# A quarter of the first product by Strassen's seven products from block 3 on, its weight sums on GpSimd, k of three tiles scaled by ScalarE

## The chip, the cores and the metric

The kernel runs on one core of a Trainium2 chip. A core has a matrix engine (PE; its weight loads are shown apart as PEld), a vector engine (DVE), a scalar engine (ACT), a general engine (GpSimd, POOL in the profile), and a queue engine (SP) that issues most DMAs. Each engine works through its own list of instructions in order, and semaphores order the engines against each other. The metric is the device time of one execution in microseconds, as the median of several runs.

## What is computed

A retention layer (attention with a decaying state) feeds a two-layer MLP with a parametric ReLU (PReLU). 4 batches, 8 heads, 768 positions, 64 values a head; 512 features, 2048 hidden ones; all inputs and the output in f32.

```python
for t in range(S):
    state = gamma[None, :, None, None] * state + np.einsum('bhd,bhe->bhde', k[:, :, t], v[:, :, t])
    y[:, :, t] = scale * np.einsum('bhd,bhde->bhe', q[:, :, t], state)
x = y.transpose(0, 2, 1, 3).reshape(B * S, H * D)          # 3072 x 512
h = x @ w_in                                               # the first product
g = np.maximum(h, 0.0) + alpha * np.minimum(h, 0.0)        # PReLU
out = g @ w_out                                            # the second product
```

## The kernel before, in words

Positions are cut into 24 tiles ("units") of 128; four units make a block of 512 tokens, and there are six blocks (n = 0 to 5). The program is written out by hand: a manual schedule, in which the order of the Python calls is the order on each engine. The two MLP products are Python generators that yield after each matmul; `tick(gen, m)` lets one go on by m matmuls, and between ticks other work is put into the queues. So the order around the change is set by the main loop at the end of the kernel alone.

Attention of one unit: `load` (L118) brings q, k and v to SBUF by SP's queue. `scaled` (L124) multiplies k or q by the decay factors from f32 to f16 (`kq`), on GpSimd as one instruction (L139) or on ACT as eight, one a head (L131). `turn` (L164) transposes `kq` by DMA to `kt`; `cast` (L152, L154) makes v f16. `prep` does all four for a unit on GpSimd. On PE, `scores` (L236) and `states` (L196) work on two units at once. On DVE, `masked` (L250) masks the scores, and `sums` (L211, L217) adds to the running state, whose decay is a multiply on GpSimd (L219). `out_first` and `out_second` (L295) make the outputs, which ACT and DVE copy to `xT`, the tokens of the next block as the first product reads them (L598, L601, L602).

The first product of a block (`ffn1`, L622) makes 16 hidden tiles of 128 x 512 tokens, four matmuls of 512 columns each. ACT makes relu(-h) (L631), and DVE's one instruction makes g from it and the PSUM bank (L632), into `gt`. The PSUM banks of these tiles take turns among four.

The second product from block 1 on (`seven`, L789) is Strassen's scheme: seven products of 16 matmuls of 256 columns instead of eight. It needs sums of `w_out` quarters (`wsum`, made once) and sums of `gt` quarters: `g_sums(n, part, which, eng)` (L739), in f16, 128 x 1024 an instruction, two parts for each of four sums. Sums 0 and 1 are chained and are DVE's; the third product needs sum 1, the fourth sum 0, the fifth sum 2, the seventh sum 3. GpSimd makes most of sums 2 and 3. Each has a tile of its own (`gs0` to `gs3`). Products leave PSUM by ACT copies (L807) and DVE adds (L819), and `out` is stored by SP.

Within block n's second product stands the attention of block n + 1: scores and states of the first pair of units, T_OUT1 matmuls, their outputs and the next pair's scores and states, T_OUT2 matmuls, that pair's outputs, and the rest of the matmuls. In `chain`, DVE does state sum, masks and state sum of a pair, with a `g_sums` on GpSimd or DVE between. All four units of block n + 1 are prepared by GpSimd during the first product of block n. Block 0 and the start are arranged otherwise and aren't touched; block 1's first product is done in two halves (L650, L664) in the midst of block 0's end.

## Time and profile before

| what | us |
|---|---|
| median of 3 runs | 198.95 |
| lowest and highest | 198.77, 200.19 |
| the profiled execution | 198.51 |
| its span in the profile | 196.5 |
| PE busy in it | 190.3 |
| DVE, ACT, POOL busy | 151.1, 98.5, 119.8 |

In the profile an instruction is named by its line, its engine, and tile written <- tiles read. The lines are those of the kernel before. In the timeline the first column is the start in us from the span's start, the second the duration of the group; x2 says that two equal ones are merged. In the groups by line the numbers behind the first bar are busy us and mean ns of one, those behind the second the idle time ahead of them.

### The profile page before, as it was taken

How to read it: one execution, taken by the hardware profiler on the slowest of the kernel's cores; microseconds unless marked ns; L12 is line 12 of the kernel's file. 1: busy time of each engine (PE TensorE's matmuls, PEld its weight loads, DVE VectorE, ACT ScalarE, POOL GpSimd, SP SyncE). 2: the span in 40 equal slices, each digit the busy share in tenths (PEclk: the TensorE clock that was granted, in tenths of full speed). 3: DMA queues.
4: the chain of work that ended last, by engine and by line, in shares of the span. 5: the costliest groups of instructions: out<-in, count | busy, mean ns of one | idle time of the engine just before them, and what ended most of it. 6: DMA issues, size and time to landing. Idle time of an engine off the chain costs nothing.

```text
span 196.5 us, 6280 instructions
## 1 busy us (share of the span) xinstructions
PE 190.3 (97%) x2632; PEld 128.9 (66%) x2632; DVE 151.1 (77%) x259; ACT 98.5 (50%) x192; POOL 119.8 (61%) x134
## 2 busy tenths in 40 slices
PE   7988999999999999999999999999999999999993
PEld 5757544558668888644888544888544888444882
DVE  2597989164989998589988589976689985789913
ACT  3378663238677925466333467234476234566110
POOL 3378989999999276994097992197971290040000
PEclk9999999999999999999999999999999999999999
DMA  5999999999998499999999999982660011300014
GB/s 157 330 358 389 407 388 329 337 332 206 209 226 188 89 291 219 226 295 257 213 228 208 286 171 251 253 208 78 180 141 0 3 57 55 109 0 3 0 53 160
DMA packets 92746, 38.75 MB, mean 197 GB/s; under 512 B 70176, under 2 KB 88624, under 8 KB 92720
## 3 DMA queue, kind: packets, MB, share of 16 engines
q1 hardware_dynamic: 91440, 37.36, 74.1%
q10 hardware_dynamic: 1280, 1.01, 1.6%
q8 instruction: 20, 0.33, 0.7%
q14 instruction: 6, 0.05, 0.1%
HBM read 27.35 MB, written 6.29 MB: 171 GB/s over the span
## 4 chain that ended last, share of the span: by engine, by line
PE 81%; DVE 9%; SPq 2%; DMA 2%; POOL 2%; issue 1%; ACT 1%; POOLq 0%
PE hps L622 33%; PE ops L789 28%; PE ops L717 5%; PE hps L650 5%; DVE gt L664 4%; SPq L342 2%; DMA qu<-in_q_dram 2%; DVE gs L739 2%; PE ops L686 2%; PE ya L524 1%; POOL gs L739 1%; PE ya L295 1%; DVE um L496 1%; PE yb L295 1%; PE sca L236 1%
## 5 line engine op out<-in xcount | busy, mean ns | idle before, releaser
L622 PE MATMUL hps<-xT,win 128*128 128x512 f16 x304 | 66.4, 379 | 0.0
L632 DVE SCALAR_TENSOR_TENSOR gt<-hm,small,hps 128x512 f16<-128x512 f32 x76 | 55.4, 745 | 8.6 <-ACT hm L631 3.5
L631 ACT ACTIVATE hm<-hps 128x512 f32<-128x512 f32 x76 | 45.4, 597 | 27.5 <-PE hps L622 27.5
L622 PEld LDWEIGHTS <-win 128*128 128x128 f16 x304 | 29.7, 98 | 34.8
L789 PEld LDWEIGHTS <-gs 128*128 128x128 f16 x320 | 30.9, 98 | 4.2 <-DVE gs L739 0.3
L139 POOL TENSOR_TENSOR kq<-kqs,tab 128x512 f16<-128x512 f32 x30 | 30.7, 1047 | 0.5 <-DMA kqs<-in_k_dram 0.3
L789 PE MATMUL ops<-wsum,gs 128*128 128x256 f16 x240 | 27.9, 273 | 0.1
L219 POOL TENSOR_TENSOR t<-ss,tab 128x256 f16<-128x256 f32 x13 | 8.4, 644 | 28.6 <-DVE ss L217 28.6
L789 PEld LDWEIGHTS <-gt 128*128 128x128 f16 x240 | 22.7, 98 | 3.4 <-DVE gt L632 0.3
L739 POOL TENSOR_TENSOR gs<-gt 128x1024 f16<-128x1024 f16 x7 | 14.9, 2130 | 14.7 <-DVE gt L632 14.7
L807 ACT ACTIVATE kept<-ops 128x512 f32<-128x512 f32 x15 | 9.0, 597 | 23.3 <-PE ops L789 23.3
L664 DVE SCALAR_TENSOR_TENSOR gt<-hm,small,hps 128x256 f16<-128x256 f32 x40 | 17.1, 476 | 4.3 <-ACT hm L659 4.2
L819 DVE TENSOR_TENSOR os<-ops,kept 128x512 f32<-128x512 f32 (+1 forms) x17 | 10.6, 626 | 11.3 <-ACT kept L807 6.3
L789 PE MATMUL ops<-wout,gt 128*128 128x256 f16 x160 | 18.5, 273 | 0.0
L650 PE MATMUL hps<-xT,win 128*128 128x256 f16 x160 | 18.3, 273 | 0.0
L650 PEld LDWEIGHTS <-win 128*128 128x128 f16 x160 | 15.4, 98 | 2.4
L659 ACT ACTIVATE hm<-hps 128x512 f32<-128x512 f32 x20 | 11.9, 599 | 5.7 <-PE hps L650 4.0
L739 POOL TENSOR_TENSOR gs<-gt,gs 128x1024 f16<-128x1024 f16 x5 | 10.6, 2129 | 3.9 <-DVE gs L739 3.9
L717 PE MATMUL ops<-wout,gt 128*128 128x512 f16 x48 | 11.4, 380 | 0.0
L394 ACT ACTIVATE ukT<-trb 128x512 f16<-128x512 f16 (+1 forms) x7 | 4.5, 657 | 11.6 <-PE trb L385 11.6
L789 PE MATMUL ops<-wsum,gt 128*128 128x256 f16 x80 | 10.2, 273 | 0.0
L356 POOL TENSOR_TENSOR ukq<-ku,tab 128x512 f16<-128x512 f32 x6 | 6.1, 1042 | 5.9 <-DMA ku<-in_k_dram 5.9
(107 smaller groups left out, 268.7 us busy)
## 6 DMA issues: line engine op xcount, KB each, us to landing
out_dram<-os SPq DMA_DIRECT2D x20, 256.0 KB, 3.2
wi<-in_moe_w_in_dram SPq DMA_DIRECT2D x8, 512.0 KB, 7.7
wo<-in_moe_w_out_dram SPq DMA_DIRECT2D x8, 512.0 KB, 8.7
kqs<-in_k_dram SPq DMA_DIRECT2D x16, 256.0 KB, 4.3
kqs<-in_q_dram SPq DMA_DIRECT2D x16, 256.0 KB, 4.4
vs<-in_v_dram SPq DMA_DIRECT2D x16, 256.0 KB, 4.6
ku<-in_k_dram SPq DMA_DIRECT2D x4, 256.0 KB, 4.2
qu<-in_q_dram SPq DMA_DIRECT2D x4, 256.0 KB, 4.6
```

The source lines that it names most:

```text
L139: eng.tensor_tensor(out=kqs[u][:, a].rearrange("p i r d -> p r i d"), in0=staged[u][nm].rearrange("p (r i) d -> p r i d", i=4), in1=tab[:, ...
L622: nc.tensor.matmul(out=hps, lhsT=w_in_all[:, hp, 128 * ft : 128 * ft + 128], rhs=xT[n][:, :, hp, :], start=(hp == 0), stop=(hp == 3),)
L631: nc.scalar.activation(out=hm, in_=hps, func=RELU, bias=0.0, scale=-1.0)
L632: nc.vector.scalar_tensor_tensor(out=gt_at(n, ft, slice(0, TB)), in0=hm, scalar=oma_sb[:, ft : ft + 1], in1=hps, op0=MULT, op1=ADD,)
L650: nc.tensor.matmul(out=hps[:, 256 * (ft - f0) : 256 * (ft - f0) + 256], lhsT=w_in_all[:, hp, 128 * ft : 128 * ft + 128], rhs=xT[n][:, half ...
L659: nc.scalar.activation(out=hm, in_=hps, func=RELU, bias=0.0, scale=-1.0)
L664: nc.vector.scalar_tensor_tensor(out=gt_at(n, f, to), in0=hm[:, at], scalar=oma_sb[:, f : f + 1], in1=hps[:, at], op0=MULT, op1=ADD,)
L717: nc.tensor.matmul(out=banks[tq], lhsT=gt_at(n, ft, slice(128 * tq, 128 * tq + 128)), rhs=w_out_all[:, ft, :], start=(ft == 0), stop=(ft = ...
L739: eng.tensor_tensor(out=out, in0=a, in1=b, op=op)
L789: nc.tensor.matmul(out=bk[:, 256 * t : 256 * t + 256], lhsT=a[:, f, 128 * t : 128 * t + 128], rhs=w[:, f, :], start=first and f == 0 and ( ...
L807: nc.scalar.activation(out=t, in_=bank, func=COPY, bias=0.0, scale=1.0)
L819: nc.vector.tensor_tensor(out=os_sb[:, at], in0=x[at.start // 256][:, at], in1=y[:, at], op=op)
```

## The change

From block 3 on the first product is done by `ffn1_mix`. It takes the hidden tiles 0, 1, 8 and 9 (a quarter of 16) by Strassen's seven products: 7 x 4 matmuls of 256 columns instead of 16 of 512. The other 12 tiles are done as before (`full`). The list MIX gives the order of the parts (0, i) and the full tiles (0). Some products add up in the same PSUM bank; three are kept in SBUF by ACT and added to by DVE (`add`). The PReLU of three of the four quarters is done from SBUF: relu by ACT, a multiply and an add by GpSimd (`ends`); the last one is done by ACT and DVE as in `full`.

It needs four sums of `w_in` quarters (`win_sum`, 128 x 1024 each, once, all on GpSimd: two ahead of block 1's second product, two during block 2's first) and four sums of `xT` (`x_sum`, 128 x 512, each block, two on DVE and two on GpSimd). Their tiles take the place of `gs2` and `gs3`, so `g_sums` 2 and 3 now overwrite parts of `gt`.

The order of other work changes with it. The first part of sum 0 of `gt` goes from DVE to GpSimd in blocks 3 to 5, the first part of sum 2 from GpSimd to DVE in block 5, and T_OUT1 is 46 instead of 44. `prep` is gone: block 2 calls its parts itself; from then on the q and k of the next block's first three units are scaled during the second product ahead (q by GpSimd, k by ACT), v is cast by ACT, and only the fourth unit is scaled by GpSimd in the mix. Loads stand behind that unit's transpose.

The diff, cut to its core:

```diff
-    T_OUT1, T_OUT2 = 44, 46
+    T_OUT1, T_OUT2 = 46, 46
...
-                sbp.tile([128, HF, 256], F16, tag=f"gs{i}", bufs=1, name=f"gs{n}{i}") for i in range(4)
+                sbp.tile([128, HF, 256], F16, tag=f"gs{i}", bufs=1, name=f"gs{n}{i}") for i in range(2)
...
-            minus(eng, sm[2][:, f], gt[:, f, t0], gt[:, f, t1])
+            minus(eng, gt[:, f, t1], gt[:, f, t0], gt[:, f, t1])
         else:
-            minus(eng, sm[3][:, f], gt[:, f8, t0], sm[1][:, f])
+            minus(eng, gt[:, f8, t0], gt[:, f8, t0], sm[1][:, f])
...
+    def win_sum(i, eng):
+        if not wins:
+            wins.append(sbp.tile([128, 2, 2, 512], F16, tag="gs2", bufs=1, name="wins0"))
+        if i == 2:
+            wins.append(sbp.tile([128, 2, 2, 512], F16, tag="ukq", bufs=2, name="wins1"))
+        a = [[w_in_all[:, 2 * l : 2 * l + 2, 1024 * j : 1024 * j + 512] for l in range(2)] for j in range(2)]
...
+    MIX = [(0, 1), (0, 2), 0, (0, 5), (0, 6), 0, (0, 7), 0, 0, (0, 4), (0, 3)] + 8 * [0]
...
+        def part(r, i):
...
+            if i in (1, 6, 7):
+                t = sbp.tile(
+                    [128, 512], FP, tag="um1" if i == 6 else "um0", bufs=2, name="kept"
+                )
+                nc.scalar.activation(out=t, in_=bk[r, "b"], func=COPY, bias=0.0, scale=1.0)
+                h[r, i] = t
+            if i in (2, 7, 3):
+                add(r, {2: 1, 7: 7, 3: 6}[i], at if i != 7 else "c")
+            if i == 4:
+                b = bk[r, "b"]
+                prelu(r, relu(b, "hm"), b, 1, 0)
+
+        def add(r, i, at):
+            nc.vector.tensor_tensor(out=h[r, i], in0=bk[r, at], in1=h[r, i], op=ADD)
+            later.append((at_step[0], r, i))
...
+        def ends():
+            while later:
+                _, r, i = later.pop(0)
+                row, half = {1: (0, 0), 7: (1, 1), 6: (0, 1)}[i]
+                hm = relu(h[r, i], "uv")
...
+                nc.gpsimd.tensor_tensor(
+                    out=hv,
+                    in0=hv,
+                    in1=oma_sb[:, f : f + 2].unsqueeze(2).to_broadcast([128, 2, 256]),
+                    op=MULT,
+                )
+                nc.gpsimd.tensor_tensor(
+                    out=gt_at(n, slice(f, f + 2), slice(256 * half, 256 * half + 256)),
+                    in0=hv,
+                    in1=v,
+                    op=ADD,
+                )
+
+        for s, step in enumerate(steps):
+            at_step[0] = s
+            yield from part(*step) if step else full()
+            if later and s - later[0][0] >= (3 if later[0][2] == 1 else 2):
+                ends()
+            if s == len(steps) - 4:
+                g_sums(n, 0, 0, nc.gpsimd if rounds == 1 else nc.vector)
+            if s == len(steps) - 2:
+                g_sums(n, 0, 1, nc.vector)
+        g_sums(n, 0, 2, nc.gpsimd if n + 1 < NBLK else nc.vector)
...
     cast(10, A)
     cast(11, A)
+    win_sum(0, G)
+    win_sum(1, G)
 
     for n in range(1, NBLK):
...
-            g_sums(n, 0, 2, nc.gpsimd)
+            g_sums(n, 0, 2, G)
+            win_sum(2, G)
+            win_sum(3, G)
+            for _ in gen:
+                pass
+        elif n > 2:
+            gen = ffn1_mix(n, MIX, 1)
+            tick(gen, 8)
+            flush(late_stores)
+            if more:
+
+                scaled(u0 + 3, "k", G)
+                scaled(u0 + 3, "q", G)
+                turn(u0 + 3)
+            for u in range(u0 + UB, min(u0 + 2 * UB, NU)):
+                load(u)
...
             if n > 1:
-                chain(pa, pq, (1, 2), None)
+                chain(pa, pq, [(1, 2, G)])
                 tick(gen, T_OUT1)
+                g_sums(n, 0, 3, G)
+                for u in nxt[0:1]:
+                    scaled(u, "k", A)
             else:
-                g_sums(n, 1, 3, nc.gpsimd)
                 tick(gen, 33)
-                chain(pa, pq, None, None)
-                g_sums(n, 0, 2, nc.vector)
-                g_sums(n, 1, 2, nc.vector)
+                chain(pa, pq)
+                g_sums(n, 1, 3, G)
+                g_sums(n, 0, 2, V)
+                g_sums(n, 1, 2, V)
                 tick(gen, 27)
...
+            tick(gen, 6)
+            for u in nxt[0:2]:
+                cast(u, A)
+            for u in nxt[1:2]:
+                scaled(u, "k", A)
+                scaled(u, "q", G)
+                turn(u)
+            for u in nxt[2:3]:
+                scaled(u, "q", G)
+            tick(gen, T_OUT2 - 6 if n > 1 else 23)
             out_first(pb, z=[ps("za"), ps("zb")])
             out_second(pb)
+            for u in nxt[2:3]:
+                scaled(u, "k", A)
+                turn(u)
+            tick(gen, 7)
+            if n > 1:
+                x_sum(n + 1, 0)
+                x_sum(n + 1, 1)
+                x_sum(n + 1, 2, G)
+                x_sum(n + 1, 3, G)
```

More of the change, by code (lines that the diff above doesn't have):

```diff
@@ L842, in seven @@
         yield from product(c, sm[0], wsum[0], True)
-        yield from product(b, sm[2], wsum[2])
+        yield from product(b, A(1, 0), wsum[2])
         u3 = kept(b, "um1")
@@ L851, in seven @@
         if end:
-            gen = product(c, sm[3], W(1, 1))
+            gen = product(c, A(0, 1), W(1, 1))
             for _ in range(HF):
@@ L859, in seven @@
         else:
-            yield from product(c, sm[3], W(1, 1))
+            yield from product(c, A(0, 1), W(1, 1))
             store()
             late_stores.append(put(0, 1, c, u2))
+    wins, xsum = [], []
+    def win_sum(i, eng):
[4 more added lines that the diff above has]
+        a = [[w_in_all[:, 2 * l : 2 * l + 2, 1024 * j : 1024 * j + 512] for l in range(2)] for j in range(2)]
+        x, y, op = (
+            (lambda: (a[1][0], a[1][1], ADD)),
+            (lambda: (wins[0][:, 0], a[0][0], SUB)),
+            (lambda: (a[0][0], a[1][0], SUB)),
+            (lambda: (a[0][1], wins[0][:, 1], SUB)),
+        )[i]()
+        minus(eng, wins[i // 2][:, i % 2], x, y, op=op)
@@ new lines, in x_sum @@
+    def x_sum(n, i, eng=nc.vector):
+        if not xsum:
+            xsum.append(sbp.tile([128, 4, 2, 256], F16, tag="gs3", bufs=1, name="xsum"))
+        t = xsum[0]
+        b = [[xT[n][:, j, 2 * l : 2 * l + 2, :] for j in range(2)] for l in range(2)]
+        x, y = (
+            (b[0][1], b[0][0]),
+            (b[1][1], t[:, 0]),
+            (b[1][1], b[0][1]),
+            (b[1][0], t[:, 1]),
+        )[i]
+        minus(eng, t[:, i], x, y)
+    MIX = [(0, 1), (0, 2), 0, (0, 5), (0, 6), 0, (0, 7), 0, 0, (0, 4), (0, 3)] + 8 * [0]
@@ L1124 @@
             for i in range(UB):
[L1125 to L1130 removed]
+                scaled(u0 + i, "k", G)
+                scaled(u0 + i, "q", G)
+                turn(u0 + i)
+                cast(u0 + i, G)
+                for u in ((), (0,), (), (1, 2, 3))[i]:
+                    load(u0 + u + UB)
                 tick(gen, (14, 14, 6, 16)[i])
                 if i in (1, 2):
[L1133 to L1134 removed]
+                    g_sums(n, 0, i - 1, V)
+            g_sums(n, 0, 2, G)
[13 more added lines that the diff above has]
+                load(u)
             for _ in gen:
```

126 lines of the change are left out of this document (97 added, 29 removed).

## The prediction

> **What bounds the kernel now.** I read the page's table of engines first, then the busy time by stage, then the chain of waits.
>
> ```profile
> span 196.5 us, 6280 instructions
> PE 190.3 (97%) x2632; PEld 128.9 (66%) x2632; DVE 151.1 (77%) x259; ACT 98.5 (50%) x192; POOL 119.8 (61%) x134
> ```
> ```profile
> 63.00:80.30 17.30, 17.25 (x386) 14.71 (x385) 15.40 (x30) 9.11 (x24) 10.73 (x10) 1.00 0.86 208
> ...
> 94.10:109.26 15.16, 15.16 (x362) 13.34 (x362) 12.29 (x23) 4.99 (x12) 9.62 (x10) 1.00 1.04 212
> 109.26:123.07 13.81, 13.81 (x73) 6.14 (x74) 11.92 (x18) 8.96 (x15) 9.29 (x10) 1.00 1.15 239
> ```
> ```profile
> 94.80 4.91 PE ops L789 x44
> 99.71 0.15 PE ya L295 x2
> ...
> 109.26 13.81 PE hps L622 x64
> ```
> The stage rows give the length, then the busy us of PE, PEld, DVE, ACT and POOL, then the granted clock. PE is never idle from block 1 on, at clock 1.00. So only fewer PE cycles can shorten the run, and every new PE wait lengthens it by its full size. A first product (L622) takes 13.81 us, 0.2158 per 128x512 matmul; the second product takes 4.91/44 = 0.1116 per 128x256 matmul.
>
> **One fact decides: DVE and GpSimd exclude each other.** Here are single sums, first on DVE (start, duration), then what GpSimd ran meanwhile.
>
> ```profile
> 32.36 2.02 DVE L739 TENSOR_TENSOR wsum<-wout 128x2048 f16<-128x2048 f16 x1
> ...
> 72.75 1.70 DVE L739 TENSOR_TENSOR gs<-gt 128x1024 f16<-128x1024 f16 x2
> ...
> 90.29 1.00 DVE L739 TENSOR_TENSOR gs<-gt 128x1024 f16<-128x1024 f16 x1
> ...
> 103.60 1.11 DVE L739 TENSOR_TENSOR gs<-gt,gs 128x1024 f16<-128x1024 f16 x1
> ...
> 119.23 0.68 DVE L739 TENSOR_TENSOR gs<-gt 128x1024 f16<-128x1024 f16 x1
> ```
> ```profile
> 10.28 1.41 POOL L356 TENSOR_TENSOR ukq<-qu,tab 128x512 f16<-128x512 f32 x1
> ...
> 31.26 2.04 POOL L356 TENSOR_TENSOR ukq<-ku,tab 128x512 f16<-128x512 f32 x2 [0.37 <-DMA ku<-in_k_dram]
> 33.26 3.02 POOL L356 TENSOR_TENSOR ukq<-qu,tab 128x512 f16<-128x512 f32 x2
> ...
> 72.92 0.99 POOL L219 TENSOR_TENSOR t<-ss,tab 128x256 f16<-128x256 f32 x1 [0.99 <-DVE ss L217]
> 75.39 0.61 POOL L219 TENSOR_TENSOR t<-ss,tab 128x256 f16<-128x256 f32 x1 [1.48 <-DVE ss L217]
> ...
> 88.61 2.13 POOL L739 TENSOR_TENSOR gs<-gt 128x1024 f16<-128x1024 f16 x1
> ...
> 103.54 0.62 POOL L219 TENSOR_TENSOR t<-ss,tab 128x256 f16<-128x256 f32 x1
> ```
> A sum of 1024 takes 0.68 on DVE with GpSimd idle (119.23). At 90.29 it took 1.00: GpSimd's sum ran to 90.74, 0.45 later, and DVE lost 0.32. At 103.60 GpSimd ran 0.56 longer and DVE lost 0.43. The loss is the overlap less 0.13 both times: DVE stands until GpSimd's instruction is done. It works the other way too: 0.99 instead of 0.61 at 72.92, behind DVE's 72.75 to 73.43; and at 33.26 the pair takes 3.02 where the pair before it took 2.04. That last place also shows who comes next: GpSimd's multiplies stood back to back, and DVE's sum got in between two of them; at 72.75 GpSimd got in between two DVE sums. So they take turns. The Trainium skill, "SBUF — State Buffer", section "SBUF: two separate sides", says that a DVE instruction with two SBUF inputs and a GpSimd instruction that reads SBUF exclude each other for the whole instruction. By that rule, without the 0.13, my seven or so blocked instructions would add up to 0.9 us more; the trace agrees on the exclusion and gives the 0.13, so I keep the trace's.
>
> DVE's PReLU (hm and a PSUM bank) is not held up: in these stretches of L632 alone, GpSimd is busy in the first and idle in the second, and DVE's share is 0.76 and 0.77.
> ```profile
> 139.00:145.00 6.00, 4.57 (x7) 1.00 0.72 176
> ...
> 168.00:180.00 12.00, 9.24 (x13) 1.00 0.07 24
> ```
>
> **The gain.** In blocks 3, 4 and 5, 16 matmuls of 512 columns become 28 of 256: 16 x 0.2158 - 28 x 0.1116 = 0.33 us each, 0.98 in all. With it the mixed first product takes 13.81 - 0.33 = 13.48.
>
> **Block 1: two w_in sums in front of DVE's.** GpSimd gets two 128x1024 sums behind the scaling that ends at 65.3 (64.27 + 1.04). There it was idle, but DVE has its four sums of the block there.
>
> ```profile
> 64.27 1.04 POOL L139 TENSOR_TENSOR kq<-kqs,tab 128x512 f16<-128x512 f32 x1 [0.18 <-DMA kqs<-in_q_dram]
> ```
> ```profile
> 66.34 0.68 DVE L739 TENSOR_TENSOR gs<-gt 128x1024 f16<-128x1024 f16 x1
> 67.06 0.69 DVE L739 TENSOR_TENSOR gs<-gs,gt 128x1024 f16<-128x1024 f16 x1
> ...
> 68.39 0.69 DVE L739 TENSOR_TENSOR gs<-gs,gt 128x1024 f16<-128x1024 f16 x1
> ...
> 71.17 0.68 DVE L250 TENSOR_TENSOR m<-scb,mi 128x512 f16<-128x512 f32 x1
> ```
> ```profile
> 68.99 3.22 PE L789 MATMUL ops<-wsum,gs 128*128 128x256 f16 x28
> 72.14 0.22 PE L295 MATMUL ya<-m,vx 64*64 64x64 f16 x2
> ...
> 78.41 1.91 PE L789 MATMUL ops<-wout,gs 128*128 128x256 f16 x16
> ```
> w_in sum 1 runs 65.3 to 67.4; DVE's first sum starts at 67.3, ends 67.95. GpSimd, waiting, is next: sum 2 runs 67.8 to 69.95. DVE's second sum ends at 70.5, the third at 71.1, the fourth at 71.85 instead of 69.08. PE's third product (68.99) needs the second sum at its start: 1.5 us; its fifth matmul (70.95) needs the fourth: 0.9. Behind these the masks come 2.77 later and PE 2.4: they just meet, 0.1. Then turns between DVE's sums for the fifth product and GpSimd's state multiply: 0.25. Further, a GpSimd sum for the seventh product (2.13) now stands behind the second state multiply instead of ahead of the first, so the third state multiply (75.39 before) ends near 79.65 and its follower on DVE near 80.05, where the outputs start at 79.7: 0.35; the last GpSimd sum ends near 81.75, where the seventh product (78.41 before) starts at 81.5: 0.25. Together 3.3; bounds 2.4 (the first two alone) and 3.9.
>
> **Block 2: the other two.** They stand behind GpSimd's sum for the fifth product, which now overwrites gt and so waits for DVE's first sum.
>
> ```profile
> 92.53 0.68 DVE L739 TENSOR_TENSOR gs<-gs,gt 128x1024 f16<-128x1024 f16 x1
> 93.13 2.71 DVE L632 SCALAR_TENSOR_TENSOR gt<-hm,small,hps 128x512 f16<-128x512 f32 x4
> ...
> 96.60 0.69 DVE L739 TENSOR_TENSOR gs<-gs,gt 128x1024 f16<-128x1024 f16 x1
> ...
> 98.67 0.68 DVE L250 TENSOR_TENSOR m<-scb,mi 128x512 f16<-128x512 f32 x1
> ```
> In times of before (block 1's delay left out): DVE's first sum 90.3 to 91.0; GpSimd's 91.0 to 93.15; DVE's second waits for it, to 93.7; w_in sum 3 to 95.7, then sum 4 to 97.8. DVE's four PReLUs end at 96.4, its third sum waits for sum 4 and ends at 98.3, its fourth at 99.0 instead of 97.29. The third product, its start 32 matmuls behind 94.80, needs it four matmuls later, at 94.80 + 36 x 0.1116 = 98.82: 0.2. The second mask comes 2.06 behind the fourth sum as before (97.29 to 99.35), at 101.1; PE, two matmuls later than before (99.71 + 0.22 + 0.2 = 100.1), waits 1.0, and 0.1 for the state behind it. Together 1.3; bounds 0.5 (had DVE slipped in ahead of sum 4) and 1.6.
>
> **Blocks 3 and 4: GpSimd's chain at the end of the mix.** Let 0 be PE's start of the mix. Sum 6 of the mix passes DVE (ends 8.9), ACT (9.55), then on GpSimd a multiply and an add of 128x512 in f32, which no row shows. The nearest row is L139 at 1.047, the largest the 1.41 of L356 beside a DVE sum; I take 1.05 each as the shape is the same.
>
> ```profile
> L139 POOL TENSOR_TENSOR kq<-kqs,tab 128x512 f16<-128x512 f32 x30 | 30.7, 1047 | 0.5 <-DMA kqs<-in_k_dram 0.3
> L631 ACT ACTIVATE hm<-hps 128x512 f32<-128x512 f32 x76 | 45.4, 597 | 27.5 <-PE hps L622 27.5
> ...
> L131 ACT ACTIVATE kq<-kqs,tab 128x64 f16<-128x64 f32 x16 | 4.0, 337 | 0.0
> ```
> ```profile
> 123.65 3.67 PE L789 MATMUL ops<-wout,gt 128*128 128x256 f16 x32
> ...
> 125.25 0.69 DVE L739 TENSOR_TENSOR gs<-gs,gt 128x1024 f16<-128x1024 f16 x1
> ...
> 127.32 0.68 DVE L250 TENSOR_TENSOR m<-scb,mi 128x512 f16<-128x512 f32 x1
> ```
> The add ends at 11.75 and GpSimd's first gt sum at 13.95. DVE comes to the sum that follows it at 14.0 (PE's 17th step ends 12.62, ACT 0.6, PReLU 0.7), with one PReLU and two sums behind it, while GpSimd has its next sum (2.13) ready. If DVE is first, GpSimd holds 14.6 to 16.75 and DVE's fourth sum ends at 18.0; if GpSimd is first, DVE's end at 18.7. Before, it ended 125.94 - 123.65 = 2.3 behind the second product's start; that start is now at 14.06, so it ends 3.95 or 4.65 behind. PE comes to the outputs 46 x 0.1116 = 5.13 behind, the second mask 2.06 behind the fourth sum: a wait of 0.9 or, with a last PReLU that is late for the second product, 1.65. I take 1.3 a block, 2.6, since 13.95 and 14.0 don't tell which. The Trainium skill, "GPSIMD Engine Reference", section "3.1 Elementwise", gives 4497 ns for an f32 add of 2048, by estimate 1.12 for 512: GpSimd would be 0.15 later and DVE first, 2.0 instead of 2.6. In block 5 GpSimd has no next sum: the fourth sum ends 3.8 behind the start, needed at 4.02: 0.
>
> **At nothing.** k by ACT: 2.0 us a tile (L131, 4.0 for two) in a stage where ACT is busy 4.99 of 15.16; if that cover went, the copies behind it would come 0.65 late. Transposes and loads move in SP's queue behind GpSimd's scaling: their users come a block later. x sums, half as long as the sums above, on both engines while PE ends the seventh product; needed 1.8 into the mix. DVE in the mix has 12 PReLUs, three adds and two halves for 16 PReLUs.
>
> **Sum.** -0.98 + 3.3 + 1.3 + 2.6 = +6.2. The profiled execution takes 198.51 around its span of 196.5, giving 204.7; the median of the runs (198.95) is 0.44 above it: 205.1.
>
> **Rivals.** (1) The sums miss each other and only the gain is left: 198.0. For it: GpSimd's idle time before 69.2. Against: DVE's four sums lie in it. It decides if GpSimd reaches w_in sum 1 by 64.2 instead of 65.3 and the second finds a place behind 69. (2) Blocks 1 and 2 collide, but the mix's GpSimd chain ends over 1.5 us sooner, so its second sum is over when DVE needs the memory: 198.95 - 0.98 + 4.6 = 202.6. Against: the chain is bound by PE's steps. (3) GpSimd's f32 pair takes twice the row: all of DVE behind it 2.1 later in three blocks, +5.4: 210.5.
>
> **Chances.** Forecast 0.62, (1) 0.10, (2) 0.20, (3) 0.06, and 0.02 for a gain above 1% that no row shows. Bounds of the sum: -0.98 + 2.4 + 0.5 + 1.8 = 3.7 and -0.98 + 3.9 + 1.6 + 3.3 = 7.8. The range, 201.5 to 207.0, takes in (2) and nearly the whole sum; it leaves out (1), (3) and the gain, 0.18. One per cent, about what a measurement can tell from no change, is 2.0 us: slower 0.88, within 0.10, faster 0.02.
>
> **What would show it.** DVE's first two sums of block 1 at some 1.6 and 2.4 us instead of 0.68; PE waiting there for gs over 2 us; mixes of 13.5 us without PE idle; waits of PE for masks in blocks 2, 3 and 4. Wrong if DVE's sums in block 1 keep 0.68 beside GpSimd's, or PE idles inside the mix.

## The result, and the profile after

| what | before | changed |
|---|---|---|
| median, us | 199.57 (4 runs, 198.77 to 201.0) | 207.18 (4 runs, 206.08 to 209.85) |
| ratio | | 1.0355, 95% interval 1.026 to 1.045 |

The changed kernel is slower by 7.6 us between the medians; the forecast was 6.2 us, 205.1. As a time, 207.18 lies 0.18 above the forecast's upper end of 207.0; as a difference to the kernel before, +7.6 lies inside it (+2.55 to +8.05 over 198.95). The ratio is that of the fast runs, without the one of 209.85, which is 1.8 per cent above the fastest. The page of the profiled execution of the changed kernel:

```profile
span 208.1 us, 6448 instructions
...
PE 193.8 (93%) x2668; PEld 132.9 (64%) x2668; DVE 161.4 (78%) x266; ACT 117.3 (56%) x257; POOL 153.3 (74%) x150
...
PEclk9999999999999957999999999999999999999999
```

GpSimd is busy 33.5 us more than before and PE, with fewer cycles to spend, 3.5 us more. The row PEclk says why the second can be: in two of the 40 slices the clock that PE was granted is 0.5 and 0.7 of full speed. This execution is the longest of the four, and 1.9 us of its 208.1 lie ahead of block 1's second product, in a part that the change doesn't touch; so a second profiled execution of the same kernel, of 205.8 us (run e11 below), stands beside it.

Busy time by stage, before (three second products, and the last one with the end; columns as in the prediction: length, then busy us of PE, PEld, DVE, ACT and POOL, then the granted clock):

```profile
65.40:80.16 14.76, 14.71 (x313) 12.63 (x305) 13.00 (x25) 7.44 (x22) 8.46 (x8) 1.00 0.79 203
...
94.73:109.10 14.37, 14.37 (x303) 12.65 (x298) 11.65 (x22) 4.43 (x12) 9.46 (x10) 1.00 1.04 212
...
123.65:138.04 14.39, 14.39 (x308) 12.66 (x301) 10.73 (x21) 4.45 (x12) 9.68 (x10) 1.00 0.69 168
...
180.79:196.47 15.68, 12.62 (x113) 10.77 (x111) 7.67 (x14) 2.39 (x4) 0.00 (x0) 1.00 0.19 67
```

After, from block 1's second product on; the stages of 14.15, 14.24 and 13.48 us are the mixes:

```profile
67.33:88.85 21.52, 17.25 (x313) 13.84 (x305) 17.43 (x25) 7.67 (x22) 16.35 (x12) 0.84 1.01 227
...
103.43:119.24 15.81, 15.07 (x302) 12.73 (x298) 13.97 (x25) 10.26 (x34) 13.59 (x12) 1.00 0.64 149
119.24:133.39 14.15, 14.15 (x142) 7.86 (x140) 12.22 (x18) 11.72 (x25) 12.85 (x11) 1.00 1.01 214
133.39:148.80 15.41, 14.82 (x309) 12.78 (x301) 13.11 (x22) 11.02 (x36) 12.90 (x11) 1.00 0.67 155
148.80:163.04 14.24, 14.24 (x143) 7.89 (x140) 12.16 (x19) 11.66 (x25) 12.48 (x11) 1.00 0.53 107
163.04:178.53 15.49, 14.92 (x309) 12.86 (x305) 13.27 (x22) 5.46 (x14) 9.41 (x8) 1.00 0.11 38
178.53:192.01 13.48, 13.48 (x79) 7.33 (x77) 11.43 (x19) 10.13 (x18) 9.77 (x9) 1.00 0.12 40
192.01:208.08 16.07, 12.58 (x113) 10.69 (x111) 8.65 (x15) 2.39 (x4) 0.87 (x1) 1.00 0.19 67
```

The same stage of run e11, block 1's second product, and the only one that differs by more than 0.02 us:

```profile
65.54:84.74 19.20, 16.43 (x307) 13.32 (x305) 16.29 (x25) 7.32 (x22) 14.41 (x12) 0.91 0.90 219
```

Length less busy PE is PE's idle time. So the account in us, against the lengths before (first products 14.55, 14.58 and 13.81 in blocks 3, 4 and 5):

| part | forecast | changed kernel | run e11 |
|---|---|---|---|
| the three mixes | -0.98 | -1.07 | -1.07 |
| block 1, second product | +3.3 (2.4 to 3.9) | +6.76 | +4.44 |
| block 2, second product | +1.3 (0.5 to 1.6) | +1.44 | +1.44 |
| blocks 3 and 4 | +2.6 (1.8 to 3.3) | +2.15 | +2.16 |
| block 5's second product and the end | 0 | +0.39 | +0.38 |
| sum | +6.2 | +9.7 | +7.4 |

Block 1 of the changed kernel, in the timeline (in brackets what the instruction waited for, and how long):

```profile
68.27 0.68 DVE L733 TENSOR_TENSOR gs<-gt 128x1024 f16<-128x1024 f16 x1
68.49 1.36 POOL L138 TENSOR_TENSOR kq<-kqs,tab 128x512 f16<-128x512 f32 x1 [2.01 <-DMA kqs<-in_q_dram]
68.98 1.42 DVE L733 TENSOR_TENSOR gs<-gs,gt 128x1024 f16<-128x1024 f16 x1
69.81 2.57 POOL L733 TENSOR_TENSOR wins<-win 128x1024 f16<-128x1024 f16 x1
70.32 2.61 DVE L733 TENSOR_TENSOR gs<-gt 128x1024 f16<-128x1024 f16 x1
...
72.46 2.44 POOL L733 TENSOR_TENSOR wins<-wins,win 128x1024 f16<-128x1024 f16 x1
72.96 2.49 DVE L733 TENSOR_TENSOR gs<-gs,gt 128x1024 f16<-128x1024 f16 x1
...
75.51 1.89 PE L783 MATMUL ops<-wsum,gs 128*128 128x256 f16 x8 [3.17 <-DVE gs L733]
```

DVE and GpSimd alternate, as forecast, but from a later start: the scaling of unit 11's q stands at 68.49, 1.16 us behind the start of the second product (67.33), where before it stood 1.13 ahead of it (64.27 against 65.40). It waited 2.01 us for its load. So three GpSimd instructions, not two, meet DVE's four sums, and the fourth sum ends 8.1 us behind the product's start instead of 3.7. PE, out of other work, stands 0.74 us (for ACT's copy of one of the seven products, which came behind a cast of v that waited 0.48 us for its load) and then 3.17 us for DVE's fourth sum. And the eight matmuls behind that take 1.89 us, where eight at the 0.1116 of before take 0.89: half the clock.

Block 3, where the mix's GpSimd chain meets DVE:

```profile
131.39 2.13 POOL L733 TENSOR_TENSOR gs<-gt 128x1024 f16<-128x1024 f16 x1
...
133.55 0.69 DVE L733 TENSOR_TENSOR gs<-gs,gt 128x1024 f16<-128x1024 f16 x1 [0.18 <-POOL gs L733]
133.60 2.63 POOL L733 TENSOR_TENSOR gt<-gt 128x1024 f16<-128x1024 f16 x1
...
134.94 1.84 DVE L733 TENSOR_TENSOR gs<-gt 128x1024 f16<-128x1024 f16 x1
...
139.00 0.22 PE L288 MATMUL ya<-m,vx 64*64 64x64 f16 x2 [0.18 <-DVE m L243]
...
139.60 0.22 PE L288 MATMUL ya<-m,vx 64*64 64x64 f16 x2 [0.34 <-DVE m L243]
```

The first of the block's four gt sums is GpSimd's here. DVE's sum behind it comes next (133.55), GpSimd's other one (133.60) stands in front of the third of the four (134.94, 1.84 instead of 0.69), and PE waits for both masks. That is the forecast's cheaper order of the two.

### The profile page after: what moved, and what is told of

Read it like the earlier page. It is cut to its first block, busy times and chain, and to the rows that moved or that the text cites. A ratio compares the mean times of both kernels' runs of the same rounds, so it can differ in the third digit from the quotient of the medians.

```text
span 208.1 us, 6448 instructions
## 1 busy us (share of the span) xinstructions
PE 193.8 (93%) x2668; PEld 132.9 (64%) x2668; DVE 161.4 (78%) x266; ACT 117.3 (56%) x257; POOL 153.3 (74%) x150
## 3 DMA queue, kind: packets, MB, share of 16 engines
q10 hardware_dynamic: 1280, 1.01, 1.5%
## 4 chain that ended last, share of the span: by engine, by line
PE 54%; DVE 23%; POOL 6%; SPq 6%; DMA 4%; ACT 2%; issue 2%; POOLq 1%; DVEq 0%
PE ops L783 20%; DVE gs L733 10%; PE hps L615 9%; PE ops L710 5%; PE hps L908 5%; SPq L335 4%; DMA wi<-in_moe_w_in_dram 4%; DVE gt L657 4%; PE hps L643 3%; PE hps L946 3%; DVE gt L625 2%; POOL gs L733 2%; DVE gt L917 2%; POOL gt L1001 2%; ACT hm L901 2%
## 5 line engine op out<-in xcount | busy, mean ns | idle before, releaser
L783 PEld LDWEIGHTS <-gt 128*128 128x128 f16 x400 | 38.3, 98 | 5.4 <-DVE gt L625 0.5
L908 PE MATMUL hps<-xT,win 128*128 128x512 f16 x144 | 33.0, 379 | 0.0
L917 DVE SCALAR_TENSOR_TENSOR gt<-hm,small,hps 128x512 f16<-128x512 f32 x36 | 26.0, 743 | 5.0 <-ACT hm L901 4.0
L783 PE MATMUL ops<-wout,gt 128*128 128x256 f16 x240 | 28.1, 273 | 0.2 <-DVE gt L625 0.2
L901 ACT ACTIVATE hm<-hps 128x512 f32<-128x512 f32 x39 | 23.2, 594 | 6.9 <-PE hps L908 6.1
L783 PE MATMUL ops<-wsum,gs 128*128 128x256 f16 x160 | 22.2, 294 | 4.2 <-DVE gs L733 3.2
L615 PE MATMUL hps<-xT,win 128*128 128x512 f16 x112 | 24.8, 379 | 0.4 <-POOL win L1071 0.4
L625 DVE SCALAR_TENSOR_TENSOR gt<-hm,small,hps 128x512 f16<-128x512 f32 x28 | 20.6, 745 | 3.7 <-ACT hm L624 1.5
L624 ACT ACTIVATE hm<-hps 128x512 f32<-128x512 f32 x28 | 16.7, 597 | 10.4 <-PE hps L615 9.7
L783 PEld LDWEIGHTS <-gs 128*128 128x128 f16 x160 | 16.1, 105 | 8.6 <-DVE gs L733 4.8
L783 PE MATMUL ops<-wsum,gt 128*128 128x256 f16 x160 | 19.0, 273 | 0.0
L733 POOL TENSOR_TENSOR gt<-gt 128x1024 f16<-128x1024 f16 x6 | 13.8, 2293 | 4.1 <-DVE gs L733 3.9
L130 ACT ACTIVATE kq<-kqs,tab 128x64 f16<-128x64 f32 x64 | 16.1, 339 | 0.1
```

What stands on the lines that cost most here:

```text
L130: eng.activation(out=kqs[u][:, a, h % 4, h // 4, :], in_=staged[u][nm][:, h, :], func=COPY, bias=0.0, scale=tab[:, H * a + h : H * a + h + 1],
L615: nc.tensor.matmul(out=hps, lhsT=w_in_all[:, hp, 128 * ft : 128 * ft + 128], rhs=xT[n][:, :, hp, :], start=(hp == 0), stop=(hp == 3),)
L624: nc.scalar.activation(out=hm, in_=hps, func=RELU, bias=0.0, scale=-1.0)
L625: nc.vector.scalar_tensor_tensor(out=gt_at(n, ft, slice(0, TB)), in0=hm, scalar=oma_sb[:, ft : ft + 1], in1=hps, op0=MULT, op1=ADD,)
L733: eng.tensor_tensor(out=out, in0=a, in1=b, op=op)
L783: nc.tensor.matmul(out=bk[:, 256 * t : 256 * t + 256], lhsT=a[:, f, 128 * t : 128 * t + 128], rhs=w[:, f, :], start=first and f == 0 and ( ...
```

## The experiments

Theory, as in the prediction: where a DVE sum and a GpSimd instruction would overlap, one of them loses that time, they take turns, and where DVE's gt sums or masks are late for it PE waits. Rivals: the cost is in the mix itself; the w_in sums cost the same wherever they stand; an effect of the chip that has no place in the sum.

**The changed kernel once more, and once more again (e1, e11).** No edit.

> The changed kernel once more, to read its stages. Both theories expect the time measured for it, about 7 us above the kernel before. Theory of turns (a DVE sum with two SBUF inputs and a GpSimd instruction stand still for each other, and take turns): against before, block 1's second product is longer by about 3.3 us, block 2's by about 1.3, those of blocks 3 and 4 by about 1 to 1.6 each, and the first products of blocks 3 to 5 are 0.33 shorter each without PE idle. Rival, the mix itself (its extra waits between PE, ACT, DVE and GpSimd): blocks 1 and 2 as before, and some 2 us more in each of the first products of blocks 3 to 5.

> The changed kernel once more beside the run before, for its profile. Theory: where GpSimd's scaling of unit 11's q starts more than 1 us behind the start of block 1's second product, PE idles for 3 us or more before the third product and the clock halves: 20 to 22 us. Where it starts ahead of it, 17.5 to 19.5 us. Rival: 20 us or more in either case. Mixes 14.15, 14.24 and 13.47 and second products 15.8, 15.4 and 15.5 as before in both.

Measured: e1 209.46 us (208.71 to 210.3) where the kernel before took 200.42, ratio 1.0449 (1.0389 to 1.0509); e11, a single execution, 205.8 us, where the kernel before took 200.55. So the same kernel stood 9.0 us above the kernel before once and 5.3 another time. From block 1's second product on all other stages agree to 0.04 us with the first profile; that one took 20.60 in e1, 19.20 in e11, 21.52 in the first profile. In e11 the q of unit 11 came in time:

```profile
65.00 1.04 POOL L138 TENSOR_TENSOR kq<-kqs,tab 128x512 f16<-128x512 f32 x1 [0.60 <-DMA kqs<-in_q_dram]
...
66.36 2.31 DVE L733 TENSOR_TENSOR gs<-gt 128x1024 f16<-128x1024 f16 x1
...
68.71 2.49 DVE L733 TENSOR_TENSOR gs<-gs,gt 128x1024 f16<-128x1024 f16 x1
```

There it stands 0.54 us ahead of the product, two DVE sums are held up and two are not, as the forecast had it, and PE idles 2.05 + 0.72 us. The stage lengths came as expected for both cases (20.60 with the q 1.07 us late, 19.20 with it early), but the clock halved in e11 too. What that costs is seen on 24 matmuls of the third and fourth products, the first from e11, the second from e3, where the clock stayed at 1.00:

```profile
72.58 4.46 PE L783 MATMUL ops<-wsum,gs 128*128 128x256 f16 x24 [0.72 <-DVE gs L733]
...
70.25 2.79 PE L783 MATMUL ops<-wsum,gs 128*128 128x256 f16 x24 [0.94 <-DVE gs L733]
```

That is 1.67 us of PE's time.

**Without the w_in sums (e2).** The four sums are left out, and their tiles are set to zero by GpSimd in block 2's first product, so a quarter of the first product is not the reference's.

```diff
-    win_sum(0, G)
-    win_sum(1, G)
...
-            win_sum(2, G)
-            win_sum(3, G)
```

> The four w_in sums are left out (their tiles are set to zero by GpSimd in block 2's first product, where DVE has no sums; so three of Strassen's products are of zeros). Theory of turns: blocks 1 and 2 are as before, 4.6 us less than the changed kernel, about 202.5; what is left over the kernel before are the 2 to 2.6 us of blocks 3 and 4 less the 1 us gain. Rival, the mix itself: the same time as the changed kernel, to within 0.5.

Measured: 202.47 us (202.1 to 204.34) against 200.42, ratio 1.0125 (1.0046 to 1.0205). Block 1's second product took 15.80 us, without a wait above 0.25. So 3.4 to 5.7 us of block 1's loss in the three profiles hang on the two sums. The other 1.04 don't; that they come from other edits (a gt sum of GpSimd now stands behind the state multiply) is argued, and unit 11's q, 0.73 us late here, holds up DVE's first sum as well (1.38 us). In block 2 this run didn't tell: 16.12 us, more than with the sums, since ACT's cast of v waits 1.64 us for a load and DVE's addition of a kept product then stands for ACT; PE waits 0.88 us for it in the seventh product. That the time came out at the 202.5 expected is therefore luck: neither block is as before.

**Each w_in sum in four pieces (e3).** DVE can come in behind 256 columns.

```diff
-        minus(eng, wins[i // 2][:, i % 2], x, y, op=op)
+        for p in range(2):
+            for c in (slice(0, 256), slice(256, 512)):
+                minus(eng, wins[i // 2][:, i % 2, p, c], x[:, p, c], y[:, p, c], op=op)
```

> The same w_in sums at the same place in GpSimd's queue, each as four instructions of 256 columns instead of one of 1024, so GpSimd has the same work and a little more overhead. Theory of turns: a DVE sum now waits for at most one piece, some 0.5 us instead of up to 2.1; in block 1 the fourth sum comes at most 1.7 late instead of 2.8, and block 1 and 2 together lose about 2.2 us instead of 4.6: some 2.4 us below the changed kernel. Rival, GpSimd's queue is simply too full (its state multiplies and later sums come late by the amount of work put ahead of them): not below the changed kernel, rather 0.3 above it for the twelve added instructions.

Measured: 203.69 us (201.36 to 205.13) against 200.42, ratio 1.0121 (1.0035 to 1.0207). Block 1 took 18.43 us though q came as late as in e1 (1.07 us behind the product's start), with the clock at 1.00 throughout; DVE's four sums took 0.68, 1.42, 1.16 and 1.04 us. Block 2 took 15.16 instead of 15.81. The same GpSimd work in smaller instructions holds DVE up less: what counts is how long one instruction keeps the other engine off. The time is 5.8 us below e1, where 2.4 were expected; part of that is the clock, which halved in e1. And the rival has a share: DVE now stands 1.68 us for GpSimd's state multiply, behind eight pieces, and PE 0.99, so block 1 still loses 3.67 us.

**The two sums of block 1 alone, in the kernel before (e4).**

```diff
...
+    win_sum(0)
+    win_sum(1)
```

> The kernel before with one part of the change alone: the first two w_in sums on GpSimd at the place they have in block 1, into a tile of their own that nobody reads. Theory (DVE's sums and GpSimd's instructions exclude each other and take turns; the new wait is paid in block 1): the second product of block 1 grows from 14.8 by 2.4 to 3.3 us with PE idle for less than 3 us in one piece, by 5 to 6.5 if GpSimd reaches the sums so late that PE idles for 3.4 us or more and the granted clock halves behind it; the other blocks keep their lengths; time 1.2 to 3.2 per cent above the kernel before. Rival (block 1 is slow because of the sums in place and the moved scalings, not of the w_in sums): block 1 within 0.5 us of 14.8, the time within 0.3 per cent of before.

Measured: 205.13 us (202.55 to 207.11) against 200.15, with no interval. The four executions go with the clock: 202.55 at a mean of 1.00, 203.95 at 0.992, 206.32 and 207.11 at 0.98. The profile is that of 203.95. All other stages from there on keep their lengths to 0.02 us; of block 1's second product, these are the wait and what follows it:

```profile
70.18:73.32 3.14, 0.61 (x5) 0.32 (x5) 3.10 (x4) 0.00 (x0) 1.20 (x1) 1.00 0.97 322
73.32:77.00 3.68, 3.68 (x19) 2.71 (x20) 3.33 (x8) 0.60 (x1) 2.69 (x2) 0.55 0.98 227
```

18.96 us, 4.20 more than before: 2.53 idle (3.14 - 0.61) and 3.68 x 0.45 = 1.66 in the second row, where PE works all the time at a clock of 0.55. The rival "the sums in place and the moved scalings" falls; two sums that nobody reads do it alone. The length is between the two ranges expected: the idle time is that of the first (2.4 to 3.3), and the clock halved all the same. What this run told against my expectation is the clock: it fell behind an idle of 2.5 us, not of 3.4.

**gt sums of blocks 3 and 4 later in GpSimd's queue (e5).** The one that met DVE there, (0, 2), goes behind the first state sum, and (0, 3) behind the second pair's masks.

```diff
-        g_sums(n, 0, 2, nc.gpsimd if n + 1 < NBLK else nc.vector)
+        if n + 1 == NBLK:
+            g_sums(n, 0, 2, nc.vector)
...
-                chain(pa, pq, [(1, 2, G)])
+                chain(pa, pq, [(0, 2, G), (1, 2, G)] if n > 2 else [(1, 2, G)])
...
-                g_sums(n, 0, 3, G)
+                if n == 2:
+                    g_sums(n, 0, 3, G)
...
-                chain(pb, pq, [], [(1, 3, V)], nxt[0:1])
+                chain(pb, pq, [], [(1, 3, V)] + ([(0, 3, G)] if n > 2 else []), nxt[0:1])
```

> In blocks 3 and 4 GpSimd's first part of sum 2 stands behind the first state multiply of the second product instead of at the end of the mix, and its first part of sum 3 behind the second pair's masks; the work is the same. Theory of turns: DVE's last three sums no longer wait for it, so the waits at the outputs of blocks 3 and 4 go, 1 to 1.3 each: 2 to 2.6 us below the changed kernel. Rival, the mix itself: no change within 0.5, since nothing inside the mix is different.

Measured: 208.75 us (206.31 to 211.53) against 200.42, ratio 1.0372 (1.0283 to 1.0461), so 0.7 us below e1 and not 2 to 2.6. In block 3 it did what it was to do: the second product took 14.34 us, as before the change, with DVE's sums at 0.69 each. That shows the cause of the loss there. In block 4 the same order cost 17.25 us: two GpSimd sums now stand ahead of the state multiply, DVE waits 2.87 us for it, PE 2.17. (In block 3 a new batch begins with the second pair, whose state sum needs no multiply.) And block 1, whose code is that of the changed kernel, took 18.56 us, with the idle time of e11 (2.90 against 2.77 us) but the clock at 1.00:

```profile
69.77:73.28 3.51, 0.61 (x5) 0.32 (x5) 3.48 (x4) 0.00 (x0) 1.57 (x1) 1.00 0.97 318
73.28:77.00 3.72, 3.72 (x133) 3.26 (x136) 3.65 (x8) 0.84 (x3) 0.95 (x2) 1.00 1.00 220
```

Behind 2.90 us of idle (3.51 - 0.61) PE did 133 matmuls in 3.72 us, many of them small ones, where e4 did 19 in 3.68. From the fifth matmul of the third product to its end the stage took 11.38 us here (73.28 to 84.66) and 12.16 in e11 (72.58 to 84.74). So of the 1.67 us of PE's time that the half clock takes, 0.8 lengthened the stage; the rest PE loses in e5 too, later in the stage, 0.24 us of it for a state sum; what the remainder stands for isn't known.

**The w_in sums ahead of unit 11's q (e10).** They no longer stand behind its load.

```diff
+    win_sum(0, G)
+    win_sum(1, G)
     scaled(11, "q", G)
...
-    win_sum(0, G)
-    win_sum(1, G)
```

> The changed kernel with block 1's two w_in sums put ahead of the scaling of unit 11's q in GpSimd's queue, so that they no longer wait for that tile's load. Theory (block 1 loses more than forecast because GpSimd stands for the load of unit 11's q and then scales it and adds both sums in front of three of DVE's sums, and because the granted clock halves behind the long idle): the first w_in sum starts behind the last sum of w_out without waiting for a load, PE's idle before the third product is under 3 us in all, block 1's second product takes 17 to 19.5 us (19.5 only with the half clock) against 20.6 and 21.5 in the two profiled runs of the changed kernel, the time 1 to 2.5 per cent over the kernel before. Rival (the load has no part in it; two sums cost that much wherever they stand): 20 to 22 us and the time of the changed kernel, 3.5 to 4.5 per cent over the kernel before.

Measured: 206.13 us (204.98 to 206.59) against 200.55, ratio 1.0263 (1.0171 to 1.0354). The first sum starts behind GpSimd's sum of w_out without a wait; PE idles 0.56 and 1.57 us; block 1's second product took 18.56 us, half the clock included:

```profile
70.54:73.27 2.73, 0.61 (x5) 0.31 (x4) 2.69 (x4) 0.00 (x0) 1.40 (x1) 1.00 0.03 7
73.27:76.50 3.23, 3.23 (x18) 2.39 (x19) 3.16 (x7) 0.60 (x1) 0.61 (x1) 0.57 0.97 316
```

The load had a part in it: with it out of the way the stage is 2.0 us shorter than in e1 and 3.0 shorter than in the first profile (where the half clock lasted twice as long). The rival of one price at every place falls. The time over the kernel before, 2.6 per cent, is a little above what I had expected at most.

**Exclusion and clock by themselves (e6).** A kernel of its own that leaves out the whole computation of the reference.

> A kernel of its own that leaves out the whole computation of the reference (its output is zeros). First DVE runs three sums of two SBUF tiles, three sums of SBUF and PSUM, three scalar_tensor_tensor of SBUF and PSUM and three copies, alone, then the same beside ten GpSimd sums of 128x1024. Theory (exclusion holds only for two SBUF inputs): beside GpSimd the first three take 2 to 3 us each instead of 0.68 and GpSimd's take turns with them; the others keep their durations within 0.1 us. Rival (any access to SBUF is shared or excluded): the others grow by more than 0.3 us as well. Then PE runs bursts of 60 matmuls, 128x512, separated by idles that grow by about 0.7 us from 1.4 us on. Theory A (the clock falls when one idle fills a whole window of about 3.4 us that runs freely): no half clock behind idles under 3.4 us, half clock always behind idles over 6.8 us, in between by chance, and the half clock lasts 3.4 us. Theory B (it falls by the length of the idle alone): one length above which every burst starts at half clock, below 3.2 us or above 3.9 us.

DVE alone (busy us and mean ns behind the first bar):

```profile
L55 DVE SCALAR_TENSOR_TENSOR dc<-fa,sc,acc 128x512 f16<-128x512 f32 x3 | 2.2, 746 | 0.1
L53 DVE TENSOR_TENSOR fb<-fa,acc 128x512 f32<-128x512 f32 x3 | 2.1, 686 | 0.1
L51 DVE TENSOR_TENSOR dc<-da,db 128x1024 f16<-128x1024 f16 x3 | 2.0, 671 | 0.1
L59 DVE COPY dc<-da 128x1024 f16<-128x1024 f16 x3 | 1.3, 427 | 0.1
```

and beside GpSimd's sums:

```profile
L64 POOL TENSOR_TENSOR pc<-pa,pb 128x1024 f16<-128x1024 f16 x9 | 20.2, 2245 | 14.5 <-DVE pb L62 13.8
L59 DVE COPY dc<-da 128x1024 f16<-128x1024 f16 x3 | 6.8, 2266 | 0.1
L51 DVE TENSOR_TENSOR dc<-da,db 128x1024 f16<-128x1024 f16 x3 | 5.6, 1865 | 0.1
L55 DVE SCALAR_TENSOR_TENSOR dc<-fa,sc,acc 128x512 f16<-128x512 f32 x3 | 2.2, 745 | 0.1
...
L53 DVE TENSOR_TENSOR fb<-fa,acc 128x512 f32<-128x512 f32 x3 | 2.0, 682 | 0.1
```

With one operand in PSUM DVE keeps its time to 0.004 us, with two in SBUF it takes 1.87 instead of 0.67 (the first of the three began ahead of GpSimd). What I had not expected: the plain f16 copy, with one SBUF input, is held up just as much, 2.27 instead of 0.43. The Trainium skill, "SBUF — State Buffer", section "Who interferes with whom", names `copy` and `cast` in their two-port modes beside the instructions with two SBUF inputs. This run agrees: 2.27 us.

Then PE's bursts. The clock in the first 3.1 to 4.4 us behind idles of 2.35, 3.13, 3.92 and 4.70 us (behind 1.57 us it was 1.00, behind 5.48 us 0.51):

```profile
64.65:68.00 3.35, 3.35 (x16) 1.56 (x16) 0.00 (x0) 0.00 (x0) 1.00 0.00 0
80.89:84.00 3.11, 3.11 (x8) 1.08 (x8) 0.00 (x0) 0.00 (x0) 0.54 0.00 0
...
99.31:102.70 3.39, 3.39 (x16) 1.56 (x16) 0.00 (x0) 0.00 (x0) 1.00 0.01 2
117.12:121.50 4.38, 4.38 (x11) 1.52 (x11) 0.00 (x0) 0.00 (x0) 0.52 0.00 0
```

An idle of 3.13 us halved the clock and one of 3.92 did not. My theory B, one length that decides, falls, and so does theory A's bound of 3.4 us. By e4, e10, e11 (halved behind 2.53, 2.13 and 2.77 us of idle, each with 0.6 us of matmuls in between) and e5 (not halved behind 2.18 + 0.72), too, the length alone doesn't decide, and when the idle falls may. The Trainium skill, "TensorE: Matmul & The Clock Gate", section "Part 1: The HAM clock gate (the "warmup" mystery)", has the clock halved by an idle window of about 3.4 us that runs freely. A place in time that decides would agree with a window that runs freely; that it be idle throughout does not agree with e10, where 2.13 us of idle in a stretch of 2.73 were enough, and there the measurement decides.

**A version without the collisions (e7), the same without the mix (e8), and a second try (e9).** e7: w_in sums on DVE, two in the prologue and two in block 0, into a tile of their own and half as long, 128x512; gt sums 2 (and 3 in block 1) in tiles of their own again; GpSimd's gt sums of blocks 3 and 4 one behind each state multiply. e8: plain first products in e7. e9: the w_in sums in gaps of DVE, the first gt sum of a mix on DVE. The half length takes nothing from the result: of the 512 columns that a w_in sum of the changed kernel covers in each of its two parts, the mix reads the first 256 alone. Sums of half the length on GpSimd, at the place of the change, were not run.

```diff
+    wins = sbp.tile([128, 4, 2, 256], F16, tag="wins", name="wins")
...
+    win_sum(0, V)
+    win_sum(1, V)
...
+    win_sum(2, V)
+    win_sum(3, V)
...
-    win_sum(0, G)
-    win_sum(1, G)
...
-            win_sum(2, G)
-            win_sum(3, G)
...
-                chain(pa, pq, [(1, 2, G)])
+                chain(pa, pq, [(1, 2, G)] if n == 2 else [(0, 2, G)])
+                if n > 2:
+                    g_sums(n, 1, 2, G)
```

> The changed kernel with its waits taken away: w_in sums on DVE in the prologue and block 0 into a tile of their own, the gt sums 2 (and 3 in block 1) into tiles of their own again, in blocks 3 and 4 GpSimd's gt sums one after each state multiply. The mixed first products stay. Theory (the change's gain is 0.33 us in each of blocks 3, 4 and 5, its loss is all from GpSimd's sums standing in front of DVE's): mixes 0.34 to 0.43 us shorter than the plain first product, block 1's second product 14.8 +- 0.3, blocks 3 and 4's second products 14.4 +- 0.3, block 2's up to 0.5 longer, time 197.8 to 199.3 where the kernel before has 199.5: ratio 0.992 to 0.999. Rival (the mix costs something besides, in the second product or at its start): ratio 1.003 to 1.02 with the second products still at 15.4.

> The kernel of the run before this (e7) with plain first products in blocks 3, 4 and 5 and without w_in sums and x sums: what the mix itself is worth. Theory: first products 14.55 in blocks 3 and 4 and 13.81 in block 5 as before, the rest as in e7, so 0.9 to 1.2 us longer than e7 and within 0.3 per cent of the kernel before. Rival (the x sums and the longer chain cost as much as the matmuls gain): the same time as e7 within 0.3 us.

> The kernel of run e7 with its new delays taken away: each w_in sum goes to a gap of DVE (after the second transposes and after the state sums of the prologue's second product, at the ends of blocks 1 and 2), the first gt sum of a mix goes from GpSimd to DVE, and in block 4 one gt sum more of the second product does. Theory (what e7 lost it lost in the prologue, 0.7 us, and where GpSimd's and DVE's sums met again, 0.4 in block 2, 1.1 in block 4): first product of block 0 to second product of block 0 as before, block 2's first product 14.6, second products of blocks 3 and 4 at 14.4 to 14.7, mixes 14.15 and 14.24, so 1.0 to 2.0 us less than e7's own 132.0 us from the start of block 1's second product to the end, and a ratio to the kernel before of 0.992 to 1.0. Rival (the mix needs GpSimd's help for DVE and pays for it wherever the sums go): again 131.5 us or more from there on, ratio 1.0 to 1.01.

Measured: e7 200.95 us, e8 200.19 us, the kernel before 200.15 us beside them; ratios 1.0023 (0.998 to 1.0066) and 1.0022 (0.9989 to 1.0055). e9 201.23 us against 199.89, ratio 1.0056 (1.0017 to 1.0095). In e7:

```profile
31.04:45.62 14.58, 14.04 (x177) 6.99 (x176) 10.07 (x14) 3.93 (x7) 14.18 (x17) 1.00 1.14 311
66.31:81.18 14.87, 14.79 (x313) 12.71 (x305) 13.08 (x25) 7.43 (x22) 9.47 (x9) 1.00 0.88 217
...
124.52:138.92 14.40, 14.40 (x308) 12.55 (x301) 11.98 (x22) 10.49 (x34) 10.62 (x10) 1.00 0.66 149
153.16:168.59 15.43, 14.85 (x309) 12.78 (x305) 12.13 (x22) 5.46 (x14) 9.85 (x8) 1.00 0.11 38
```

Block 1 (14.87) and block 3 (14.40) are as before the change, and the mixes keep their gain (14.15, 14.24, 13.48). But the w_in sums now cost 0.7 us in block 0's second product (14.58 where it was 13.85), and block 4 took 15.43: GpSimd has one gt sum more to make in the second product than before, and the fifth product waits 0.38 us for it. Block 2's second product is back at 14.32 us, but its first took 14.87 (14.57 before), and the last stage 16.25 (15.68 before). e8 was to be 0.9 to 1.2 us longer than e7; it isn't, by the ratios or the medians: what the mixes gain, their sums cost again. e9 took away the delay in block 0 (13.95) and lost in the second products of blocks 2, 3 and 4 (15.12, 14.79 and 16.00) what it gained; its profile is of the longest of its twelve executions. From block 1's second product to the end it took 133.6 us, and its ratio lies in the range of its rival, 1.0 to 1.01. So neither the theory's range (0.992 to 0.999) nor the rival's cause (second products at 15.4 everywhere) holds for e7: the collisions can be taken out of blocks 1 and 3, but the sums have to stand somewhere, and on engines as busy as these every place I tried cost at least the 1.07 us that the mixes gain. No version faster than the kernel before was found; that there is none is not shown.

## Why the prediction was right, and where a size was off

The direction, the mechanism and the places were right, and the sum was near: +6.2 forecast, +7.6 between the medians. How near is in part luck: beside e1 the same kernel was 9.0 us slower, which is above the sum's upper bound of 7.8, and the gap is nearly all in one term, block 1. By its own steps:

- **The gain.** -0.98 forecast, -1.07 measured (0.40, 0.34 and 0.33), and PE doesn't idle in the mixes. Right; so the gain was where the diff says, and is small.
- **Block 1.** +3.3 forecast (2.4 to 3.9), +4.44, +5.84 and +6.76 in the three profiles. The step that was mis-sized. Its working took GpSimd to reach the first w_in sum at 65.3, as the one profile of before shows it, 0.1 us ahead of the start of the second product. Where GpSimd came about there the waits were as forecast: DVE's first two sums took 2.31 and 2.49 us in e11 and 2.40 and 2.49 in e5 (1.6 and 2.4 forecast), and PE idled 2.77 us and 3.20 us in that stage; in e5, with the clock at 1.00, the stage took 18.56 us, +3.80 and so inside the bounds. Two things were not in the sum. GpSimd can come to unit 11's q up to 2.3 us later against the product's start than in the profile of before, since it stands for loads (2.01 us for that q in the first profile; 1.3 for earlier tiles and 0.33 for that q in e1); then a third GpSimd instruction is in the way and PE idles 3.9 us. And the clock halves behind the idle, where the prediction let a wait of PE cost its own length and no more: 1.7 us of PE's time in e4 and e11, of which 0.8 stays in the stage by e5, and 2.54 in the first profile (17.25 - 14.71). It is no rare event: the mean clock of an execution is 0.983 to 0.992 in all nine of the changed kernel, and 0.998 to 1.00 in the fourteen of the kernel before beside e1 and e11. The term's upper bound should have taken in both.
- **Block 2.** +1.3 forecast, +1.44 measured. 0.74 of it is idle PE, above all at the masks (0.19 and 0.34); the rest lies in PE's busy time, 0.31 of it in the third product, whose weight loads wait for the sum. So the waits at the masks are smaller than the 1.0 forecast, and the total is right rather than its parts. The turns came out as forecast: DVE's second sum stands for GpSimd's gt sum (1.61 us), its third for the second w_in sum (1.95).
- **Blocks 3 and 4.** +2.6 forecast, +2.15 measured. The order between 0.9 and 1.65 a block that 13.95 and 14.0 didn't tell apart came out as the cheaper one (1.02 and 1.13): DVE's sum goes first. GpSimd's f32 add, which no row of before showed, took 1.27 us instead of the 1.05 assumed, the multiply 1.04:

```profile
L1001 POOL TENSOR_TENSOR gt<-hm,kept 128x512 f16<-128x512 f32 x9 | 11.5, 1274 | 0.7
...
L995 POOL TENSOR_TENSOR hm<-hm,small 128x512 f32<-128x512 f32 x9 | 9.3, 1039 | 3.7 <-ACT hm L901 3.7
```

  So GpSimd's first gt sum ended 0.33 us later than forecast (14.28 into the mix, at 133.52), and DVE, which waited for it, went first. The Trainium skill's "GPSIMD Engine Reference", section "3.1 Elementwise", gives 4497 ns for 2048, by estimate 1.12 us for this add; that is below the measured 1.27, though its order of the two, DVE first, is the one that came.
- **Block 5.** 0 forecast, +0.38 measured. About 0.1 us of it lies in the third product, which needs the gt sums. Most of the rest is the last store, which lands 2.89 us behind DVE's last addition (2.58 before); it took 2.57 in e3, with the same code there. What sets that is open.
- **The rivals.** "The sums miss each other" fell by DVE's sums of 2.3 to 2.6 us. "Blocks 1 and 2 only" fell by block 3 (15.41, and 14.34 in e5 with the sum moved). "GpSimd's f32 pair takes twice the row" fell by 1.04 and 1.27.

Why the clock halves in one execution and not in another with the same idle time could be a window that runs freely; that is argued, not shown, since no run sets the window's phase.

## What to carry to other kernels

Work given to an engine that is idle is not free when it shares a resource with the engine it relieves: lay the GpSimd instructions in time beside DVE's SBUF-to-SBUF ones, with who comes next, before counting the matmuls saved. Where such an instruction must stand ahead of critical sums, make it no longer than what is read of it (not tried here on GpSimd), cut it in pieces, and take the load in front of it into the bounds, for it moves from execution to execution. And an idle PE can cost more than its length: behind idles of 2.1 us and more in this kernel, allow for the half clock, which took 1.7 us of PE's time and made the stage 0.8 longer.

## What the runs showed that was not expected

- Behind PE idles of 2.13 to 3.9 us the granted clock was 0.5 for some 3.4 us in e4, e10, e11 and e1 (24 matmuls took 4.46 us instead of 2.79) and for 6.8 us in the first profile, and it was 1.00 in e5 behind 2.90 us. In e6, 3.13 us halved it and 3.92 us did not.
- A DVE f16 copy of 128x1024 takes 2.27 us beside GpSimd's sums instead of 0.43, as if it had two SBUF inputs; the instructions with a PSUM operand lose nothing (0.682 and 0.745 us beside them, 0.686 and 0.746 alone).
- GpSimd's scaling of one q tile, behind loads, stood between 0.54 us ahead of block 1's second product and 1.16 us behind its start in executions of the same code.
